# Splitting the 512-column matmuls of one stage into two of 256 columns, in a kernel of Fourier transforms and a feed-forward block

## The chip, the core and the metric

One core of one Trainium2 chip runs the kernel. The metric is the device time of one execution in microseconds (us); the kernel before took 2559.97 us in the median of three runs (2555.99 to 2562.64).

## What is computed

The reference takes x of 8 batches by 3008 places by 256 channels. Along the 3008 places it makes a real Fourier transform, multiplies each frequency by one complex 256 x 256 matrix, adds a bias, pulls real and imaginary parts towards zero by 0.01 and transforms back. A feed-forward block follows on all 24064 rows.

```
X = rfft(x, axis=1)
Yr = Xr @ w_r - Xi @ w_i + b_r
Yi = Xr @ w_i + Xi @ w_r + b_i
Y  = sign(Y) * max(|Y| - 0.01, 0)        (for Yr and Yi)
y  = irfft(Yr + 1j * Yi, n=3008, axis=1)
h  = y @ w_in                            (256 -> 2048)
out = (h * clip(h + 3, 0, 6) / 6) @ w_out  (2048 -> 256)
```

## The kernel before

3008 is 64 times 47, so each transform is made of a 47-point and a 64-point one, and each of these is a matmul with a table of sines and cosines. The work of a batch goes through these steps:

- `stage1`: the forward 47-point transform, 7 loads of x, to a scratch tensor in DRAM (`scr1`).
- `middle`, in 12 groups `g`: `s2` is the forward 64-point transform, `s3` the product with the 256 x 256 weights, the bias and the shrinking, `s4` the split of its result into a high and a low part, and `s5` the inverse 64-point transform, whose result `pt` goes to a second scratch tensor (`scr2`).
- `segment`: the inverse 47-point transform, 7 segments, from `scr2` through the tile `qt` into `raw`.
- The feed-forward block, in 47 chunks of 512 columns, of 8 units each. Its first layer (`phase_a` to `phase_d`, tiles `pb`, `pc`, `pd`) takes seven products of 256 columns in place of eight; its second (`down`, tile `po`) gives each weight to two matmuls of 256 columns.

Most products are made of values split in two (`split`, L133 to L137): a high part of a shorter type and the rest. `product` (L147) then issues three matmuls for each pair of operands: rest times high, high times rest, high times high, all into the same place of PSUM.

The step of the change is `s5` (L494). Batch 0 takes another form. For batches 1 to 7 it issues through `product` three matmuls, each 128 x 128 weights by 512 columns, into one bank of PSUM (`ps_a`, 128 x 512, two buffers): first with the weights `g_lo`, then twice with `g_hi`; the moving operand is the two halves of `z`. That is 84 groups and 252 matmuls. Each matmul has one load of its weights. The flag `whole` hands the three to `together` (L139), which lets no other matmul of TensorE come between them. ScalarE then copies the bank to `pt` (L500), and SyncE's queue stores it (L501).

The order within each engine is not that of the code: a scheduler plans it when the kernel is built, with a model of how long each instruction takes, and writes one list for each engine. The code sets priorities, and the places at which steps of `stage1`, `middle` and `segment` may enter between those of the feed-forward block (`lay`, `fill`). So an instruction whose modelled length changes can change the order of all that comes after it.

Of the kernel before, what the change touches and what calls it, by code (L numbers as in the profile page):

```python
# [101 lines left out]
def spectral_ffn(ctx: ExitStack, tc: tile.TileContext, x, w_r, w_i, bias, w_in, w_out, f47, f64, g64, sgn, out):  # L102
# [12 lines left out]
    def space(shape, dt, name, tag=None):  # L115
        tag = tag or name
        return sb.tile(shape, dt, name=name, tag=tag, bufs=depth.get(tag, 1))
# [6 lines left out]
    def room(wide=False):  # L124
        if wide:
            return ps_b.tile([P, 512], F32, name="pb")
        return ps_a.tile([P, 512], F32, name="ps_a")
# [11 lines left out]
    def together(matmuls):  # L139

        first, *rest = [functools.partial(nc.tensor.matmul, **m) for m in matmuls]
        first = first()  # L142
        with tc.high_priority(), tc.issue_after(first.ins):
            for m in rest:
                m()  # L145

    def product(ps, terms, start=True, stop=True, more=False, whole=False):  # L147

        todo = [p for (ah, al), (bh, bl) in terms for p in ((al, bh), (ah, bl), (ah, bh))]
        matmuls = [  # L150
            dict(
                out=ps,
                lhsT=a,
                rhs=b,
                start=start and n == 0,
                stop=stop and n == len(todo) - 1,
                skip_group_check=more,
            )
            for n, (a, b) in enumerate(todo)
        ]  # L160
        if whole:
            together(matmuls)
        else:
            for m in matmuls:
                last = nc.tensor.matmul(**m)  # L165
            return last
# [133 lines left out]
    def stage1(b):  # L300
# [17 lines left out]
        for i, (n1, n) in enumerate(sets):  # L318
# [8 lines left out]
            for c, src in enumerate((e, plus)):  # L327
                q = 2 * i + c
                if whole:
                    ps = idle(q) if b else room(c == 1)  # L330
                    turns = f47_s[2][:rows, c * R47 : c * R47 + rows]
                    nc.tensor.matmul(out=ps[:rows, :w], lhsT=turns, rhs=src, start=True, stop=True)
                else:
                    xs = [t[:rows, :w] for t in twin([P, 2 * D], F32R, "xs")]
                    split(*xs, src, nc.gpsimd)
                    yield
                    ps = room()
                    product(ps[:rows, :w], [([t[:rows, c * R47 : c * R47 + rows] for t in f47_s[:2]], xs)], whole=True)
                home = ("a", "h", "z", "h", "xs", "h", "X")[q % 7] if b == 0 else "yb" if whole else "a"
                a = space([P, 2 * D], F32, "a", home)[:rows, :w]  # L340
                if home == "X":
                    space([P, 48], F32, "gap")
                nc.scalar.copy(out=a, in_=ps[:rows, :w])
                dst = scr1[b][c, n1 : n1 + n].rearrange("(g j) k d -> (j k) g d", g=w // D)
                stores.append(nc.sync.dma_start(out=dst, in_=a.rearrange("p (g d) -> p g d", d=D)))
                if c and i + 1 < len(sets) and i + 1 >= len(shapes) and not whole:
                    shapes.append(load(i + 1))
                yield
# [40 lines left out]
    g64_s = g64_t[:2]  # L389
# [6 lines left out]
    def middle(b):  # L396
# [5 lines left out]
        bt, xs, zs = {}, {}, {}  # L402

        def tag(g, *tags):

            return tags[0 if b else g % 3]
# [34 lines left out]
        def mixed(ps, x, *terms):  # L441
            product(
                ps,
                [
                    (tuple(t[:, dh, which] for t in x), part(w_s[w], slice(dh * D, (dh + 1) * D)))
                    for which, w in terms
                    for dh in range(2)
                ],
            )
# [42 lines left out]
        def s5(g):  # L492
            ps = room(b == 0)
            flat = lambda t: t.rearrange("p k d -> p (k d)")  # L494
            if b:
                product(ps, [(g64_s, [flat(t) for t in zs.pop(g)])], whole=True)
            else:
                nc.tensor.matmul(out=ps, lhsT=g64_t[2], rhs=flat(zs.pop(g)), start=True, stop=True)
            pt = space([P, 2, D], F32, "pt", tag(g, "pt", "ot", "ot"))
            nc.scalar.copy(out=pt, in_=ps.rearrange("p (k d) -> p k d", d=D))  # L500
            nc.sync.dma_start(out=dst[:, 2 * g : 2 * g + 2, :], in_=pt)  # L501
# [3 lines left out]
        for g in range(NG + LAG[2]):  # L505
            if g >= LAG[2]:
                s5(g - LAG[2])
                yield
            if b and 0 <= g - LAG[1] < NG:
                s4(g - LAG[1])  # L510
            if 0 <= g - LAG[0] < NG:
                s3(g - LAG[0])
            if 0 <= g - LAG[0] < NG + 1:
                yield
            if g < NG:
                s2(g)
                yield
# [73 lines left out]
    def prepare(c):  # L591
        y = raw.pop(c)
        b11, b12, b21, b22 = y[:, 0, :H], y[:, 0, H:], y[:, 1, :H], y[:, 1, H:]
        s = space([P, 4, H], F32, "T")
        for to, p, q in ((0, b12, b11), (1, b22, s[:, 0]), (2, b22, b12), (3, b21, s[:, 1])):
            (nc.gpsimd if c else nc.vector).tensor_tensor(out=s[:, to], in0=p, in1=q, op=ALU.subtract)
        yield
        for n, src in ((2, b21), (1, b11), (6, s[:, 1]), (7, s[:, 2]), (5, s[:, 0]), (4, s[:, 3]), (3, b22)):
            t = space([P, 2, H], F32R, "yb")
            with behind(("h", c * nf - 1 if n == 3 else -1)):  # L600
                split(t[:, 0], t[:, 1], src, nc.gpsimd if c else nc.vector)
            yb[c, n] = (t[:, 0], t[:, 1])
            yield
# [184 lines left out]
    for c in range(1, NC):  # L788
        g = prepare(c)
# [111 lines left out]
```

## Time and profile before

| | before |
|---|---|
| median of three runs | 2559.97 us |
| the profiled execution | 2560.95 us |
| its span, first to last instruction | 2559.2 us |
| TensorE matmuls: busy, number | 2502.8 us (98%), 20910 |
| TensorE weight loads: busy | 2447.6 us (96%) |
| VectorE, ScalarE, GpSimd: busy | 77%, 71%, 30% |
| mean granted TensorE clock | 0.988 |

The profile of one execution lists every instruction with its start and its length. TensorE (PE) has two lists there, matmuls and weight loads (PEld); both are pipelined, so one instruction's length is longer than the distance to the next one's start, and it is the distance that sets the time. "ps_a<-z,g_hi" is a matmul that writes tile `ps_a` from the moving or stationary operands `z` and `g_hi`. L142 and L145 are the two lines of `together`, L165 is `product`, L711 is `down`.

### The profile page before, as it was taken

To read this page: it belongs to the slowest core of one execution; us is meant where nothing else is said; L and a number is where in the kernel's file an instruction comes from. 1 tells how busy PE (TensorE), PEld (TensorE's weight loads), DVE (VectorE), ACT (ScalarE), POOL (GpSimd) and SP (SyncE) were. 2 spreads that over 40 slices of the span, in tenths; PEclk is the share of its full clock that TensorE was granted. 3 is DMA by queue.
4 is the path that set the end of the run, shared out by engine and by line. 5 is a ranking of instruction groups with operands and counts; after the bars stand their busy time and mean duration, and the time that the engine had idled before them with its cause. 6 is when DMAs were issued, how large, how long until landed. Compare 5 with 4: busy or idle time off the path is not lost.

```text
span 2559.2 us, 53456 instructions
## 1 busy us (share of the span) xinstructions
PE 2502.8 (98%) x20910; PEld 2447.6 (96%) x20910; DVE 1965.0 (77%) x3191; ACT 1825.9 (71%) x3587; POOL 756.2 (30%) x738
## 2 busy tenths in 40 slices
PE   6789999999999999999999999999999999999999
PEld 4579999999999999999999999999999999999999
DVE  7778878877787777777787777777777778677766
ACT  5467777777777777777777777777777777777776
POOL 3253342333223332323323333223321221121310
PEclk8889999999999999999999999999999999999999
DMA  7733432332222222333222222222222121110000
GB/s 244 224 88 103 126 103 83 91 91 68 60 84 78 86 72 67 85 86 89 60 75 84 72 79 84 71 78 80 74 78 59 53 66 51 37 41 17 12 18 17
DMA packets 150259, 200.54 MB, mean 78 GB/s; under 512 B 16863, under 2 KB 104215, under 8 KB 150007
## 3 DMA queue, kind: packets, MB, share of 16 engines
q1 hardware_dynamic: 150007, 197.13, 26.7%
q8 instruction: 164, 2.69, 0.5%
q14 instruction: 88, 0.72, 0.1%
HBM read 97.45 MB, written 74.97 MB: 67 GB/s over the span
## 4 chain that ended last, share of the span: by engine, by line
PE 90%; DMA 3%; DVE 3%; ACT 1%; POOL 1%; issue 1%; SPq 1%; ACTq 0%; POOLq 0%; DVEq 0%
PE po L711 38%; PE pb L165 19%; PE pc L165 10%; PE ps_a L145 7%; PE ps_a L165 7%; PE pd L165 5%; PE ps_a L142 3%; DMA xin<-in_x 1%; DMA zt<-tc 1%; DMA qt<-scr 0%; DMA x_lo<-in_x 0%; DVE r L682 0%; ACT r L680 0%; POOL e L325 0%; ACT gs L136 0%
## 5 line engine op out<-in xcount | busy, mean ns | idle before, releaser
L711 PE MATMUL po<-gs,w_out_hi 128*128 128x256 f32 x5984 | 1025.6, 277 | 0.0
L711 PEld LDWEIGHTS po<-gs,w_out_hi 128*128 128x128 f32 x5984 | 839.2, 188 | 1.6
L682 DVE SCALAR_TENSOR_TENSOR r<-r,h 128x1024 f32<-128x1024 f32 x375 | 476.4, 1270 | 269.4 <-ACT r L680 267.4
L711 PE MATMUL po<-gs,w_out_lo 128*128 128x256 f32 x2992 | 594.8, 278 | 0.9 <-ACT gs L136 0.5
L680 ACT ACTIVATE r<-h,three 128x1024 f32<-128x1024 f32 x375 | 433.0, 1155 | 191.5 <-DVE h L621 189.4
L165 PE MATMUL pb<-yb,w_in_hi 128*128 128x256 f32 x3008 | 568.2, 278 | 0.0
L137 DVE TENSOR_TENSOR gs<-r,gs 128x1024 fp32r<-128x1024 f32 x375 | 483.5, 1289 | 90.9 <-ACT gs L136 87.1
L136 ACT CAST gs<-r 128x1024 fp32r<-128x1024 f32 x375 | 394.3, 1051 | 109.3 <-DVE r L682 106.6
L165 PEld LDWEIGHTS pb<-yb,w_in_hi 128*128 128x128 f32 x3008 | 458.1, 189 | 3.1
L711 PEld LDWEIGHTS po<-gs,w_out_lo 128*128 128x128 f32 x2992 | 456.0, 188 | 3.8 <-ACT gs L136 2.2
L165 PE MATMUL pb<-yb,w_in_lo 128*128 128x256 f32 x1504 | 426.3, 286 | 2.0 <-ACT u L616 1.3
L137 POOL TENSOR_TENSOR yb<-T,yb 128x256 fp32r<-128x256 f32 x184 | 168.3, 917 | 841.9 <-ACT yb L136 828.2
L621 DVE TENSOR_TENSOR h<-pc,u 128x256 f32<-128x256 f32 x752 | 314.2, 418 | 113.1 <-PE pc L165 106.8
L616 ACT COPY u<-pb 128x256 f32<-128x256 f32 x752 | 279.5, 373 | 94.4 <-PE pb L165 80.5
L165 PE MATMUL pc<-yb,w_in_hi 128*128 128x256 f32 x1504 | 295.7, 278 | 0.0
L165 PEld LDWEIGHTS pb<-yb,w_in_lo 128*128 128x128 f32 x1504 | 283.5, 189 | 8.7 <-ACT u L616 2.8
L165 PEld LDWEIGHTS pc<-yb,w_in_hi 128*128 128x128 f32 x1504 | 228.9, 189 | 0.7
L165 PE MATMUL pc<-yb,w_in_lo 128*128 128x256 f32 x752 | 214.6, 285 | 4.7 <-DVE h L621 4.6
L616 ACT COPY p<-pb 128x256 f32<-128x256 f32 x376 | 140.1, 373 | 77.0 <-PE pb L165 75.1
L654 ACT COPY h<-pb 128x256 f32<-128x256 f32 x376 | 141.3, 376 | 49.4 <-PE pb L165 47.6
L621 DVE TENSOR_TENSOR h<-pd,p 128x256 f32<-128x256 f32 x376 | 156.6, 417 | 13.9 <-ACT p L616 11.8
L165 PEld LDWEIGHTS pc<-yb,w_in_lo 128*128 128x128 f32 x752 | 141.9, 189 | 9.4 <-DVE h L621 8.1
(165 smaller groups left out, 3939.4 us busy)
## 6 DMA issues: line engine op xcount, KB each, us to landing
bt<-scr SPq DMA_DIRECT2D x96, 256.0 KB, 3.0
scr<-pt SPq DMA_DIRECT2D x96, 256.0 KB, 2.4
zt<-tc SPq DMA_DIRECT2D x376, 64.0 KB, 2.0
out<-ot SPq DMA_DIRECT2D x93, 256.0 KB, 2.3
scr<-a SPq DMA_DIRECT2D x96, 240.0 KB, 2.7
qt<-scr SPq DMA_DIRECT2D x96, 240.0 KB, 3.5
xin<-in_x SPq DMA_DIRECT2D x42, 480.0 KB, 4.4
f<-in_f SPq DMA_DIRECT2D x96, 128.0 KB, 2.8
```

Source lines behind the costliest of these rows:

```text
L136: nc.scalar.copy(out=hi, in_=src)
L137: (on or nc.vector).tensor_tensor(out=lo, in0=src, in1=hi.bitcast(F32), op=ALU.subtract)
L142: first = first()
L145: m()
L165: last = nc.tensor.matmul(**m)
L616: nc.scalar.copy(out=t, in_=ps)
L621: nc.vector.tensor_tensor(out=to, in0=ps, in1=keep.pop((i, n)), op=ALU.add)
L654: marks["h", i] = nc.scalar.copy(out=hs[i][:, 1, :H], in_=pb)
L680: nc.scalar.activation(out=r, in_=h, func=AF.Relu, bias=three, scale=1.0)
L682: nc.vector.scalar_tensor_tensor(out=r, in0=r, scalar=6.0, in1=h, op0=ALU.min, op1=ALU.mult)
L711: last = nc.tensor.matmul(out=pos[dh][half], lhsT=w[:, ft * D + dh * P : ft * D + (dh + 1) * P], rhs=g[:, low, u, cols], start=opens and n ...
```

## The change

`product` gets a flag `paired`, and `s5` sets it for batches 1 to 7. Each 512-column matmul of the group becomes two, for columns 0 to 255 and 256 to 511, which follow each other with the same weights; each of the two has its own weight load. Only the first matmul of the six opens the bank (`start`).

```
-    def product(ps, terms, start=True, stop=True, more=False, whole=False):
+    def product(ps, terms, start=True, stop=True, more=False, whole=False, paired=False):
...
+        if paired:
+            matmuls = [
+                dict(
+                    m,
+                    out=m["out"][:, cols],
+                    rhs=m["rhs"][:, cols],
+                    start=m["start"] and cols.start == 0,
+                    skip_group_check=True,
+                )
+                for m in matmuls
+                for cols in (slice(0, 256), slice(256, 512))
+            ]
         if whole:
             together(matmuls)
...
-                product(ps, [(g64_s, [flat(t) for t in zs.pop(g)])], whole=True)
+                product(ps, [(g64_s, [flat(t) for t in zs.pop(g)])], whole=True, paired=True)
```

The change adds 12 lines above all but the first of the lines that are named here, so that L165 reads L177 in the lists of the changed kernel, L501 L513, L711 L723, and so on.

**TensorE at the first group of batch 1.** The list before, with the semaphores that a matmul waits for in brackets:

```order
L165 MATMUL pb<-yb,w_in_lo 128x256 [waits Activation_49]
L165 MATMUL pb<-yb,w_in_hi 128x256 x2
L142 MATMUL ps_a<-z,g_lo 128x512 [waits Activation_49]
L145 MATMUL ps_a<-z,g_hi 128x512 x2
L165 MATMUL pc<-yb,w_in_lo 128x256 [waits DVE_49]
L165 MATMUL pc<-yb,w_in_hi 128x256 x2
L711 MATMUL po_2205<-gs,w_out_lo 128x256 [waits Activation_49]
```

And of the changed kernel:

```order
L177 MATMUL pb<-yb,w_in_lo 128x256 [waits Activation_49]
L177 MATMUL pb<-yb,w_in_hi 128x256 x2
L142 MATMUL ps_a<-z,g_lo 128x256 [waits Activation_49]
L145 MATMUL ps_a<-z,g_lo 128x256
L145 MATMUL ps_a<-z,g_hi 128x256 x4
L177 MATMUL pc<-yb,w_in_lo 128x256 [waits DVE_49]
L177 MATMUL pc<-yb,w_in_hi 128x256 x2
L723 MATMUL po_2205<-gs,w_out_lo 128x256 [waits Activation_49]
```

Three rows became six at the same place, with the same wait at the first; nothing else moved here, and nothing ahead of this group.

**TensorE at the second group.** Before:

```order
L142 MATMUL ps_a<-z,g_lo 128x512 [waits DVE_49,PE_49]
L145 MATMUL ps_a<-z,g_hi 128x512 x2
L711 MATMUL po_2205<-gs,w_out_hi 128x256 x2
L711 MATMUL po_2210<-gs,w_out_hi 128x256 x2
L165 MATMUL pc<-yb,w_in_lo 128x256 [waits DVE_49]
L165 MATMUL pc<-yb,w_in_hi 128x256 x2
L165 MATMUL pd<-yb,w_in_lo 128x256
L165 MATMUL pd<-yb,w_in_hi 128x256 x2
L165 MATMUL ps_a<-w_r_hi,X 128x256 [waits DVE_49]
```

And now:

```order
L142 MATMUL ps_a<-z,g_lo 128x256 [waits DVE_49,PE_49]
L145 MATMUL ps_a<-z,g_lo 128x256
L145 MATMUL ps_a<-z,g_hi 128x256 x4
L723 MATMUL po_2205<-gs,w_out_hi 128x256
L177 MATMUL pc<-yb,w_in_lo 128x256 [waits DVE_49]
L177 MATMUL pc<-yb,w_in_hi 128x256 x2
L723 MATMUL po_2205<-gs,w_out_hi 128x256
L723 MATMUL po_2210<-gs,w_out_hi 128x256 x2
L177 MATMUL ps_a<-w_r_hi,X 128x256 [waits DVE_49]
```

The product into `pc`, which waits for VectorE, moved ahead of three matmuls of the second layer, and the product into `pd` behind the start of `s3`. Such small moves go on to the end of the list.

**SyncE's queue at the first segment of batch 3.** The names carry buffer numbers; the tensor `scr2_8836` (`scr2_8908` after) holds that batch, and `qt_13189` (`qt_13297`) takes its first two parts. Before:

```order
L501 DMA scr2_8836<-pt_12868 128x512
L732 DMA out_0<-ot_12803 128x512
L531 DMA qt_13189<-scr2_8836 120x2x256
L732 DMA out_0<-ot_12808 128x512
L410 DMA bt_13150<-scr1_9247 128x512
L411 DMA f64_13151<-in_f64 128x256
L531 DMA qt_13189<-scr2_8836 120x2x256
```

And now:

```order
L513 DMA scr2_8908<-pt_12976 128x512
L543 DMA qt_13297<-scr2_8908 120x2x256 x2
L744 DMA out_0<-ot_12913 128x512
L744 DMA out_0<-ot_12908 128x512
L422 DMA bt_13258<-scr1_9319 128x512
L423 DMA f64_13259<-in_f64 128x256
```

Both loads of `qt` now stand ahead of the two stores of the output. Of the 1063 transfers of this queue 91 stand at another place than before, by at most 6 places; on ScalarE it is 1451 of 3589 instructions, by at most 11, on VectorE 1036 of 3193, by at most 9, on GpSimd 32 of 743.

## Rows read from the trace of the kernel before

**Rows 1.** The page, part 1: busy time of each engine.

```profile
PE 2502.8 (98%) x20910; PEld 2447.6 (96%) x20910; DVE 1965.0 (77%) x3191; ACT 1825.9 (71%) x3587; POOL 756.2 (30%) x738
```

**Rows 2.** Busy time by stretch (from:to us), with the granted TensorE clock (PEclk).

```profile
200.00:2205.00 2005.00, 2000.62 (x17055) 1975.17 (x17055) 1568.44 (x2567) 1461.17 (x2898) 609.36 (x585) 1.00 0.27 78
2205.00:2555.00 350.00, 349.30 (x2984) 347.08 (x2982) 243.80 (x371) 244.63 (x453) 67.30 (x74) 1.00 0.07 23
```

**Rows 3.** Waits of TensorE's matmuls from 200 to 2205 us: total, times, longest.

```profile
PE ps_a L145 <- DMA qt<-scr: 1.1, 1, 1.1
PE ps_a L142 <- DVE raw L574: 1.1, 1, 1.1
...
PE ps_a L142 <- DVE r L682: 0.5, 2, 0.3
```

**Rows 4.** Instructions that touch z: count, min/median/max ns; then who waited for them (us, times).

```profile
L145 PEld LDWEIGHTS ps_a<-z,g_hi x168: 187/188/192, 226.1 to 2204.3; 128*128 128x128 f32 x168
L145 PE MATMUL ps_a<-z,g_hi x168: 387/393/403, 226.4 to 2204.6; 128*128 128x512 f32 x168
...
L142 PE MATMUL ps_a<-z,g_lo x84: 388/390/502, 226.1 to 2204.1; 128*128 128x512 f32 x84
...
  ACT pt L500: 11.0, 20
```

**Rows 5.** Timeline of matmuls around one group: start us, us, what.

```profile
503.87 0.39 PE L711 MATMUL po<-gs,w_out_hi 128*128 128x256 f32 x2
504.10 0.28 PE L165 MATMUL pc<-yb,w_in_lo 128*128 128x256 f32 x1
...
504.89 0.39 PE L142 MATMUL ps_a<-z,g_lo 128*128 128x512 f32 x1
505.12 0.62 PE L145 MATMUL ps_a<-z,g_hi 128*128 128x512 f32 x2
505.58 0.28 PE L165 MATMUL pb<-yb,w_in_lo 128*128 128x256 f32 x1
505.70 0.40 PE L165 MATMUL pb<-yb,w_in_hi 128*128 128x256 f32 x2
505.93 0.28 PE L165 MATMUL pb<-yb,w_in_lo 128*128 128x256 f32 x1
506.06 0.39 PE L165 MATMUL pb<-yb,w_in_hi 128*128 128x256 f32 x2
```

**Rows 6.** Timeline of weight loads just ahead of the same group.

```profile
504.33 0.53 PEld L711 LDWEIGHTS po<-gs,w_out_hi 128*128 128x128 f32 x4
504.78 0.19 PEld L142 LDWEIGHTS ps_a<-z,g_lo 128*128 128x128 f32 x1
```

**Rows 7.** Chain of waits in three stretches: start us, us, what.

```profile
505.74 0.71 PE pb L165 x6
...
2176.57 1.02 PE ps_a L165 x9
2177.59 0.68 PE pb L165 x6
...
2274.51 1.81 PE po L711 x16
...
2449.36 1.88 PE po L711 x16
```

**Rows 8.** Groups of matmuls by form: 2262 to 2282, 2482 to 2540, 200 to 2205, 2205 to 2560 us.

```profile
L711 PE MATMUL po<-gs,w_out_hi 128*128 128x256 f32 x66 | 11.5, 276 | 0.0
...
L711 PE MATMUL po<-gs,w_out_hi 128*128 128x256 f32 x162 | 29.3, 281 | 0.0
...
L711 PE MATMUL po<-gs,w_out_hi 128*128 128x256 f32 x4874 | 835.2, 277 | 0.0
...
L711 PE MATMUL po<-gs,w_out_hi 128*128 128x256 f32 x1008 | 172.7, 279 | 0.0
```

**Rows 9.** Waits of SyncE's queue from 200 to 2560 us.

```profile
SPq L531 <- PE pb L165: 232.7, 26, 25.4
...
SPq L732 <- ACT ot L729: 138.2, 24, 42.0
```

## The prediction

> **What bounds the kernel now.** I began with the busy times of the engines [rows 1]: TensorE's matmuls fill 98% of the span, its weight loads 96%, VectorE 77%. A share alone doesn't say that TensorE is the limit, so the stretches come next [rows 2]. From 200 to 2205 us, which holds every group that changes (the first matmul of them starts at 226.1, the last at 2204.6 [rows 4]), matmuls are under way for 2000.62 of 2005 us. What is left, 4.4 us, is made of single waits of about a microsecond [rows 3]. After 2205 it is 349.30 of 350. The granted clock is 1.00 in both, the 2.4 GHz level, so there is no clock to win or lose while TensorE stays as busy as that. The reader should see that nothing else matters here: time changes only if the distance between starts of TensorE's matmuls changes, or if TensorE waits more or less.
>
> So the number to read is that distance, not the length in the tables. A 256-column matmul is 276 ns long [rows 8], but sixteen of them take 1.81 us in the chain [rows 7]: 0.113 us each. In the timeline, seven of 256 columns lie between 504.10 and 504.89, again 0.113 each; the three of 512 columns take from 504.89 to 505.58, 0.69 us or 0.230 each [rows 5]. A 512-column matmul therefore takes twice a 256-column one and a little more: both go by columns.
>
> There is a second pace: elsewhere sixteen of the same matmuls take 1.88 us, 0.118 each [rows 7]. The mean length tells which pace a stretch had: 276 ns at 0.113, 281 at 0.118 [rows 8]. From 200 to 2205 it is 277, mostly the short pace; after 2205 it is 279, so over half at the long one.
>
> **The change, part by part.**
>
> *The 252 matmuls become 504.* A group takes 0.69 us now; six at 0.113 take 0.68. That is 0.01 less for each of 84 groups: **-0.9 us**.
>
> *The matmuls behind a group.* After the three of 512 columns, the next four of 256 take from 505.58 to 506.06, 0.48 us where four at 0.113 take 0.45 [rows 5]; in the chain the six behind a group take 0.71 where six take 0.68 elsewhere [rows 7]. So each group leaves some 0.03 us behind it. A group of 256-column matmuls does not: behind the nine of `s3` the six into `pb` take 0.68 [rows 7]. If the new groups behave like those, 84 x 0.03 = **-2.5 us**. The other bound is 0, should the trail come from the bank or from `z` and not from the width. I take -2.5, as the nine of `s3` write the same tile and differ in the width.
>
> *The 252 added weight loads.* One is 188 ns long [rows 4]. If none were hidden they would cost 252 x 0.188 = 47 us; if all are, 0. Four loads in a row take 0.53 us in all [rows 6], 0.188 and three times 0.113, so a load overlaps the one before it and keeps pace with 256-column matmuls. More than 17,000 pairs run that way [rows 2], and I take **0**. The cover is thin: weight loads are under way for 1975 of 2005 us [rows 2].
>
> *The long pace.* I can't see what ends it; it may be an interruption of the even stream, such as a 512-column matmul. A mean of 277 between 276 and 281 puts up to a fifth of 2005 us at the long pace, which costs 0.2 x 2005 x (1 - 0.113/0.118) = 17 us; the trails are 2.5 of that. Groups of 512 columns also stand in `stage1`, and the short ones of `s2` and `segment` interrupt as well, so the group of `s5` is one of four kinds. Were the long stretches a third longer, it would cost +4 to +5; the lower bound is 0. I take **+1**, near the lower end, since those of the trails cannot grow.
>
> *The order.* The planner's lists differ from the second group on, by a few places on each engine. ScalarE's copy to `pt` waited for the group 20 times, 11.0 us in all [rows 4], and stands right behind it as before. Of SyncE's queue, a load of `qt` that stands behind a store waits for the store's own wait first (24 waits of stores for ScalarE, 138.2 us in all, as against 232.7 for `qt` on TensorE [rows 9]). At the first segment of batch 3 both loads now precede the stores, which can only bring `qt` earlier, and the stores wait for nothing later on. But TensorE waited for `qt` once in 2005 us, 1.1 us [rows 3], so little can be won. Elsewhere such a wait can appear. I take **0**, with -5 (all idle time gone) to +5 (as much again) as bounds.
>
> The sum is -0.9 - 2.5 + 0 + 1 + 0 = -2.4 us. The profiled execution took 2560.95 us, so 2558.5; the median of the three runs is 1.0 below that execution, and by it the sum is 2557.6. I forecast **2558 us**.
>
> *A rule that speaks against the change.* The row gives 0.113 against 0.230 us, so two halves cost no more than the whole. The Trainium skill, page "TensorE: Matmul & The Clock Gate", section "Back-to-back issue gap", gives a warm matmul its columns at 2.4 GHz and 2.5 ns on top, so every split pays 2.5 ns again; by that page's figures my estimate is that the 252 splits cost +0.6 us in place of -0.9, and the sum would be 1.5 us higher. The trace disagrees with its figures (0.113 where it has 0.109, 0.230 where it has 0.216), and I go by the trace.
>
> **The rivals.**
>
> 1. *The long pace holds on (slower).* If the 512-column groups are what returns TensorE to the short pace, then without 84 of them it stays long after each disturbance. For it: after 2205 us, where none of these groups stand, over half of the time is at the long pace [rows 8]. Against: that stretch also lacks `s2`, `s3` and `stage1`. If half of 2005 us ran at it, 0.5 x 85 = 42 us would be lost, 2600 us in all. It decides from 8 us on, which is a further tenth of the 2005 us at the long pace; I would then expect about 2570.
>
> 2. *The new order is luckier (faster).* The long stretches after 2205 us cost 0.6 x 350 x 0.042 = 9 us, and the idle time in the two stretches is 5 us. An order that by chance enters the long pace less often at the end and drops the waits gives up to -14 beside the -3.4 above: 2544; half of it, 2550. For it: the order there does change. Against: it may as well go the other way, and is not aimed at.
>
> 3. *The loads are not hidden (slower).* Each second half waits for its own load. The price is up to 47 us, 2606; at half of that 2582. Against it stand the four loads in 0.53 us [rows 6]. The skill's page, in the same section, also has a sustained figure for streams of load and matmul, 131 ns at 512 columns against 81 at 128; an estimate from that page, read linearly, is 98 at 256, so that a split costs 64 ns, 16 us for 252, or 2577. The 0.230 us for 512 columns [rows 5] contradicts it.
>
> 4. *Nothing happens.* If the trail stays, or the repeated load of the same weights behaves as the single one did, the time is 2559 to 2561, no change. For it: by columns the work is the same.
>
> **How the numbers follow.** About 0.3%, 7.7 us, is what a measurement of this kernel can tell from no change; the three runs lie within 6.7 us of each other. My forecast has 0.63, and nothing happening 0.22, both within that bound. Rival 1 has 0.06 and rival 3 has 0.02, both slower by more. Rival 2 has 0.07; the larger part of it, or the whole with the gain above, is faster by more. That gives faster 0.07, same 0.85, slower 0.08. The range runs from 2551, where rival 2 begins to be large, to 2566, which takes in the order's +5 and some of the long pace's +4.
>
> **What would show it.** In the profile after, the six matmuls of a group should take 0.68 us, and the next six 0.68 where it was 0.71; the count of matmuls and loads should be 21162 each, and the loads 188 ns long. The mean length from 200 to 2205 us should stay at 276 to 277 ns: if it rises to 278 or more, rival 1 is right, and the chain will show 1.88 us for sixteen in the middle of the run. If TensorE's idle time there is over 10 us, the order is to blame. A group of over 0.8 us would mean rival 3.

## The result, and the profile after

The changed kernel takes 2571.17 us in the median of five runs (2569.45 to 2574.7), the kernel before 2557.7 us in five runs beside them (2555.99 to 2562.64): a ratio of 1.0054, 95% interval 1.0042 to 1.0065. The change makes the kernel slower by some 13.5 us, which lies outside the range that was forecast. The profiled executions lie closer together, 2570.76 against 2560.95 us, since that of before was one of its longer ones.

Page, part 1, and busy time by stretch of the changed kernel (columns as in [rows 2]):

```profile
PE 2505.9 (98%) x21162; PEld 2463.4 (96%) x21162; DVE 1969.1 (77%) x3191; ACT 1827.1 (71%) x3587; POOL 764.2 (30%) x738
```

```profile
200.00:2205.00 2005.00, 1999.74 (x17185) 1985.99 (x17185) 1565.03 (x2547) 1452.98 (x2876) 606.49 (x577) 1.00 0.27 78
2205.00:2565.00 360.00, 358.12 (x3091) 354.74 (x3089) 251.45 (x388) 253.27 (x474) 78.32 (x81) 1.00 0.07 22
```

The 252 added matmuls and loads are there. TensorE is as busy as before [rows 2] and its clock is at the same level, 1.00. It should have done more in 2005 us if nothing had got slower: 84 groups bring 252 more instructions, but only 130 more lie in that stretch than before. Idle time is 5.3 us where it was 4.4. So the loss is in the distance between matmuls while TensorE counts as busy.

Timeline of matmuls around one group, answering to [rows 5]:

```profile
506.33 0.62 PE L723 MATMUL po<-gs,w_out_hi 128*128 128x256 f32 x4
506.78 0.28 PE L142 MATMUL ps_a<-z,g_lo 128*128 128x256 f32 x1
506.89 0.28 PE L145 MATMUL ps_a<-z,g_lo 128*128 128x256 f32 x1
507.01 0.62 PE L145 MATMUL ps_a<-z,g_hi 128*128 128x256 f32 x4
507.46 0.28 PE L177 MATMUL pb<-yb,w_in_lo 128*128 128x256 f32 x1
507.58 0.40 PE L177 MATMUL pb<-yb,w_in_hi 128*128 128x256 f32 x2
507.82 0.28 PE L177 MATMUL pb<-yb,w_in_lo 128*128 128x256 f32 x1
507.93 0.40 PE L177 MATMUL pb<-yb,w_in_hi 128*128 128x256 f32 x2
508.17 0.28 PE L177 MATMUL pd<-yb,w_in_lo 128*128 128x256 f32 x1
```

The six matmuls of the group take from 506.78 to 507.46, 0.68 us: 0.113 each, as forecast. The six behind it take from 507.46 to 508.17, 0.71: 0.118 each. So far this is the trail of before. But it doesn't end. The chain of waits in the same place, and later in the run:

```profile
507.62 0.71 PE pb L177 x6
508.33 0.35 PE pd L177 x3
508.69 0.71 PE ps_a L177 x6
509.39 0.35 PE pc L177 x3
509.75 1.53 PE po L723 x13
...
1948.14 1.89 PE po L723 x16
```

Nine matmuls into `ps_a` and `pc` behind it take 1.06 us and thirteen into `po` 1.53, all at 0.118; around 1948 us sixteen take 1.89, where [rows 7] have 1.81 and 1.88 for the two paces. The groups of matmuls by form say the same of whole stretches, 200 to 2205 us and then 2205 us to the end (answering to the last two lines of [rows 8]):

```profile
L723 PE MATMUL po<-gs,w_out_hi 128*128 128x256 f32 x4835 | 834.0, 278 | 0.0
...
L723 PE MATMUL po<-gs,w_out_hi 128*128 128x256 f32 x1045 | 177.3, 277 | 0.0
```

The mean rose from 277 to 278 in the first and fell from 279 to 277 in the second. A mean of whole nanoseconds is too coarse for a price, so I counted the distances between the starts in the timeline, for 256-column matmuls. I call 116 to 130 ns the long pace, take its cost as what is over 113.3 ns, and count all above 130 ns as waits:

| | long pace, 190 to 2205 us | its cost | long pace, 2205 to 2555 us | its cost | waits, cost in both |
|---|---|---|---|---|---|
| before | 1435 of 15323 | 6.9 us | 1669 of 2877 | 7.5 us | 30.4 us |
| after | 4758 of 15715 | 21.8 us | 659 of 2909 | 3.0 us | 32.9 us |

The long pace costs 14.9 us more where the groups are and 4.5 less behind them, and waits 2.5 more; the three are 12.9 us. What lies outside the table (matmuls of other widths, the start and the end of the run) gives some 3 us back. The difference of the two profiled executions is 9.8.

Where the long pace begins and ends can be counted by groups. I take the groups behind which at least 14 matmuls of the feed-forward block follow before a group of another stage. Such a group leaves the long pace behind if most of the seventh to fourteenth distances there are long, and it found the long pace if most of the six distances of the feed-forward block ahead of it were long. From 190 to 2205 us, 1 of 50 groups of `s5` left the long pace behind before, and 39 of 53 do after. It ends at two other stages: of the groups that found it in the changed kernel, all 12 of `stage1` and all 12 of `segment` left the short pace behind, but only 1 of 26 of `s3`.

### The profile page after: what moved, and what is told of

Read it like the earlier page. It is cut to its first block, busy times and chain, and to the rows that moved or that the text cites. A ratio compares the mean times of both kernels' runs of the same rounds, so it can differ in the third digit from the quotient of the medians.

```text
span 2569.0 us, 53979 instructions
## 1 busy us (share of the span) xinstructions
PE 2505.9 (98%) x21162; PEld 2463.4 (96%) x21162; DVE 1969.1 (77%) x3191; ACT 1827.1 (71%) x3587; POOL 764.2 (30%) x738
## 4 chain that ended last, share of the span: by engine, by line
PE 91%; DMA 3%; DVE 2%; ACT 2%; POOL 1%; issue 1%; SPq 0%; ACTq 0%; DVEq 0%
PE po L723 39%; PE pb L177 19%; PE pc L177 10%; PE ps_a L145 8%; PE ps_a L177 7%; PE pd L177 5%; PE ps_a L142 3%; DMA zt<-tc 1%; DMA x_lo<-in_x 0%; DVE r L694 0%; DMA xin<-in_x 0%; ACT r L692 0%; DMA st<-in_w_out 0%; DVE w_in_lo L137 0%; POOL m L242 0%
## 5 line engine op out<-in xcount | busy, mean ns | idle before, releaser
L723 PE MATMUL po<-gs,w_out_hi 128*128 128x256 f32 x5984 | 1029.3, 277 | 0.0
L723 PEld LDWEIGHTS po<-gs,w_out_hi 128*128 128x128 f32 x5984 | 841.2, 188 | 0.7
L694 DVE SCALAR_TENSOR_TENSOR r<-r,h 128x1024 f32<-128x1024 f32 x375 | 482.7, 1287 | 253.1 <-ACT r L692 251.5
L723 PE MATMUL po<-gs,w_out_lo 128*128 128x256 f32 x2992 | 597.0, 278 | 1.5 <-ACT gs L136 1.1
L177 PE MATMUL pb<-yb,w_in_hi 128*128 128x256 f32 x3008 | 571.9, 278 | 0.0
L177 PEld LDWEIGHTS pb<-yb,w_in_hi 128*128 128x128 f32 x3008 | 459.1, 189 | 1.6
L723 PEld LDWEIGHTS po<-gs,w_out_lo 128*128 128x128 f32 x2992 | 456.4, 188 | 4.2 <-ACT gs L136 3.2
L177 PE MATMUL pb<-yb,w_in_lo 128*128 128x256 f32 x1504 | 427.1, 286 | 3.5 <-ACT u L628 2.3
L177 PE MATMUL pc<-yb,w_in_hi 128*128 128x256 f32 x1504 | 296.5, 278 | 0.0
L177 PEld LDWEIGHTS pb<-yb,w_in_lo 128*128 128x128 f32 x1504 | 283.6, 189 | 8.5 <-ACT u L628 4.2
L177 PEld LDWEIGHTS pc<-yb,w_in_hi 128*128 128x128 f32 x1504 | 229.3, 189 | 0.6
L177 PE MATMUL pc<-yb,w_in_lo 128*128 128x256 f32 x752 | 214.6, 285 | 8.0 <-DVE h L633 7.9
L137 POOL TENSOR_TENSOR xs<-xin,xs 120x512 fp32r<-120x512 f32 (+1 forms) x45 | 60.4, 1341 | 328.2 <-ACT xs L136 320.8
```

Source lines behind the costliest of these rows:

```text
L137: (on or nc.vector).tensor_tensor(out=lo, in0=src, in1=hi.bitcast(F32), op=ALU.subtract)
L694: nc.vector.scalar_tensor_tensor(out=r, in0=r, scalar=6.0, in1=h, op0=ALU.min, op1=ALU.mult)
L723: last = nc.tensor.matmul(out=pos[dh][half], lhsT=w[:, ft * D + dh * P : ft * D + (dh + 1) * P], rhs=g[:, low, u, cols], start=opens and n ...
```

## The experiments

Three theories stood at the start. A: something in or behind a split group leaves TensorE at the long pace. B: another property of the group does (its operands, its length). C: the planner's new order causes it through waits. Each expectation says anew what A, B and C stand for in its run. The runs of the kernel before beside the experiments had medians of 2558.16, 2556.78 and 2557.12 us in the three sets.

### First set: order, width and stage

**The halves in turn.** All three products for columns 0 to 255, then all for 256 to 511:

```
-                for m in matmuls
                 for cols in (slice(0, 256), slice(256, 512))
+                for m in matmuls
```

> The six matmuls of a group in another order: columns 0 to 255 with g_lo, g_hi, g_hi, then columns 256 to 511 with g_lo, g_hi, g_hi, so that no weights are loaded four times in a row and the halves of the bank don't alternate. Theory A (a group of 256-column matmuls with these operands leaves TensorE at the 0.118 us pace, whatever their order): about 2571 us, and the matmuls behind a group stay at 0.118. Theory B (the pace is set off by the alternating halves or the repeated weights): about 2557 us, and the matmuls behind a group run at 0.113. Theory C (the planner's new order costs the 13 us through waits, the pace is a by-thing): 2566 to 2574, as the order is nearly that of the change, with waits of TensorE 3 us or more above the kernel before.

2569.26 us, ratio 1.0047 (1.0032 to 1.0063). Neither the alternating halves nor the weights repeated four times matter; the theories A and C are left, as both expected this time.

**The last matmul left whole.**

```
-                for m in matmuls
+                for m in matmuls[:-1]
                 for cols in (slice(0, 256), slice(256, 512))
-            ]
+            ] + [dict(matmuls[-1], skip_group_check=True)]
```

> Only the first two matmuls of a group are split; the third stays at 512 columns. Theory A (a 512-column matmul at the end of a group lets TensorE return to 0.113 after some five matmuls, a 256-column one doesn't): 2555 to 2560 us, and a trail of about five slower matmuls as in the kernel before. Theory B (any split of the group sets off the long pace and nothing at its end helps): about 2571. Theory C (the planner's order): 2565 to 2573.

2574.78 us, ratio 1.0066 (1.0051 to 1.0081), the opposite of what theory A expected. Chain of waits around one group, five matmuls of which the last has 512 columns:

```profile
608.92 0.11 PE ps_a L142
609.03 0.57 PE ps_a L145 x4
609.60 0.35 PE po L723 x3
...
610.07 0.35 PE pc L177 x3
610.42 0.59 PE pb L177 x5
611.01 0.59 PE po L723 x5
```

Sixteen matmuls later TensorE is still at 0.118. A 512-column matmul does not bring the short pace back by its width. That part of rival 1's explanation does not hold for this group.

**Both stages split**, the groups of `stage1` as well, so that no 512-column matmul is left in batches 1 to 7:

```
-                    product(ps[:rows, :w], [...], whole=True)
+                    product(ps[:rows, :w], [...], whole=True, paired=w == 512)
```

> The change, and also the 512-column matmuls of stage1 in batches 1 to 7 (26 groups of three in two thirds of the batches, 78 groups in all) are split in the same way. Theory A (512-column groups are what ends the long pace in the middle of the run): the long pace lasts longer, 2580 to 2595 us, mean matmul length from 200 to 2205 us at 279 or more. Theory B (each split group changes the pace from one to the other, also back): more changes but about as much time at either, 2568 to 2580. Theory C (order alone): within 5 us of the change, 2566 to 2576.

2579.01 us, ratio 1.008 (1.0064 to 1.0097): at the upper end of B's range and 1 us short of A's, whose sign, a mean of 279, doesn't come (it is 278). 6265 of 16080 distances up to 2205 us are at the long pace. The split groups of `stage1` end it less often: 10 of the 14 that found it, where it was 12 of 12.

**Only `stage1` split**, the groups of the inverse transform as before.

> The kernel before with the 512-column matmuls of stage1 split in place of those of the inverse 64-point transform. Theory A (a split group of any stage leaves TensorE at 0.118): slower than before, 2565 to 2572 us, and the matmuls behind a stage1 group run at 0.118. Theory B (the operands of the inverse transform, g and z, set it off, not the width): 2555 to 2560 us, and 0.113 behind a stage1 group, without the trail. Theory C (order alone): 2553 to 2570, either way.

2557.1 us, ratio 1.0003 (0.9993 to 1.0012). Splitting 512 columns costs no time that the interval shows in the other stage: six matmuls into `ps_a` with `xs` leave a trail of three or four and no more. The chain around one such group:

```profile
499.05 0.12 PE ps_a L142
499.17 0.59 PE ps_a L145 x5
499.76 0.58 PE pb L177 x5
500.34 0.45 PE po L723 x4
500.79 0.11 PE pb L177
500.90 1.70 PE po L723 x15
```

The fifteen at the end are at 0.113. So it is not width alone but something about the group of `s5`.

### Second set: places in SBUF

What differs are the operands, and they differ in one thing that no row shows: where they stand. As the tiles are laid out, the weights of the feed-forward layers and, in batches 1 to 7, `X`, the stationary operand of `s3`, start at 160 modulo 256 bytes, and their moving operands (`yb`, `gs`, the 256 x 256 weights) at 96. In the group of the change it is the other way round: `g_hi` and `g_lo` at 96, `z` at 160. Two pads in the code can be moved to change that without touching any instruction. The pad behind `g64` goes ahead of it, and the order in which batch 0 first asks for three tiles decides on which side of the other pad `z` stands:

```
+        const.tile([P, 16], F32, name="last")
         g64_t = loaded(g64, P, P, "g64")
         nc.sync.dma_start(out=sgn_s, in_=sgn)
-        const.tile([P, 16], F32, name="last")
...
-                home = ("a", "h", "z", "h", "xs", "h", "X")[q % 7] if b == 0 else ...
+                home = ("a", "h", "X", "h", "z", "h", "xs")[q % 7] if b == 0 else ...
```

The operations of TensorE, ScalarE and SyncE are then, row for row, those of the kernel from which it is made, so the planner's order is held fixed. The first hunk alone is the first run of this set, the second alone the fourth, both together the second and, on the kernel before, the third.

> The change with one thing moved in SBUF: the tables g_hi, g_lo stand 64 bytes later, at 160 modulo 256 bytes, where the weights of the feed-forward layers and of s3 stand too; z stays at 160. The order on every engine is that of the change, row for row. Theory A (where stationary and moving operand stand in SBUF sets the pace: elsewhere weights are at 160 and the moving operand at 96, in this group it is the other way round, and each such turn switches between 0.113 and 0.118): something changes behind the groups; if the two together count, the group is now half turned and the time lies anywhere from 2553 to 2571; if the weights alone count, 2553 to 2560. Theory B (the operands g and z in themselves, or the length of the group): 2567 to 2573. Theory C (the planner's order): 2567 to 2573, as the order is the same.

> The change with z (and xs) at 96 modulo 256 bytes, g_hi and g_lo left at 96; the order on every engine is that of the change. Theory A: if the two together count, half turned, 2553 to 2571; if the moving operand alone counts, 2552 to 2560 and the first of these runs stays at 2571; if the weights alone count, 2567 to 2573. Theory B and theory C: 2567 to 2573.

> The change with g_hi, g_lo at 160 modulo 256 bytes and z at 96, as weights and moving operands stand in the other groups; xs moves to 96 too, other tiles but X keep their places, and the order on every engine is that of the change. Theory A (places in SBUF): no change of pace behind a group, 2552 to 2559 us, mean matmul length from 200 to 2205 us back at 276 to 277. Theory B (the operands or the length of the group): 2567 to 2573. Theory C (the planner's order): 2567 to 2573.

> The kernel before, 512 columns in a group, with the same places as the last: g_hi, g_lo at 160, z and xs at 96 modulo 256 bytes; its order on every engine is its own. Theory A (places): the trail of some five slower matmuls behind a group goes as well, 84 times some 0.02 to 0.03 us, 2553 to 2558 us. Theory B (the trail comes from 512 columns): trail and time as before, 2556 to 2561. Theory C says nothing of it but no change.

| columns in a group | g at, z at (modulo 256) | median us | ratio to before, interval | long pace, 190 to 2205 us |
|---|---|---|---|---|
| 256 (the change) | 96, 160 | 2571.17 | 1.0054, 1.0042 to 1.0065 | 4758 of 15715 |
| 256 | 160, 160 | 2561.39 | 1.0014, 1.0004 to 1.0024 | 2166 of 15806 |
| 256 | 160, 96 | 2557.76 | 0.9999, 0.9988 to 1.001 | 1932 of 15797 |
| 256 | 96, 96 | 2575.08 | 1.0072, 1.0055 to 1.0089 | 5847 of 15665 |
| 512 (before) | 96, 160 | 2556.78 | 1 | 1435 of 15323 |
| 512 | 160, 96 | 2573.6 | 1.0064, 1.0048 to 1.008 | 4904 of 15184 |

The chain of waits behind a group with both moved, 256 columns:

```profile
525.47 0.11 PE ps_a L142
525.58 0.57 PE ps_a L145 x5
526.15 0.68 PE pb L177 x6
526.83 0.34 PE pd L177 x3
527.17 0.34 PE pc L177 x3
527.51 2.38 PE po L723 x21
```

Everything behind it here runs at 0.113: no trail, and no long pace. With the same matmuls in the same order as the change, 64 bytes in the places of the operands take the 13.5 us away. That settles it against theory C. The same places under the kernel before do the opposite; the chain behind a group of three 512-column matmuls:

```profile
527.55 0.23 PE ps_a L142
527.77 0.47 PE ps_a L145 x2
528.24 0.71 PE pb L165 x6
528.95 0.35 PE pd L165 x3
529.30 0.35 PE pc L165 x3
529.65 1.41 PE po L711 x12
```

Now the unsplit group stays at 0.118. I had expected its trail to go, and it became endless: a miss, and the most telling run. At these places the split is worth 2573.6 - 2557.8 = 16 us; at the places of before it costs 13.5. The value of the change has no sign of its own.

The rows of the table with 256 columns tell more than their times. Here are the group and a piece behind it with `g` alone moved, and then with `z` (and `xs`) alone moved:

```profile
527.36 0.59 PE ps_a L145 x5
...
529.33 1.25 PE po L723 x11
```

```profile
531.11 0.60 PE ps_a L145 x5
...
533.12 0.94 PE po L723 x8
```

In both the group itself is slow, 0.118 or more per matmul; in the median it takes 0.707 and 0.717 us, where it takes 0.682 with the operands at 96 and 160 and 0.680 at 160 and 96. So in the two rows where both stand at the same place, the group has the long pace; most of its own matmuls are then among the long ones of the table. But what it leaves behind differs: 0.114 with `g` alone moved, 0.118 with `z` alone moved. Counted as above, 2 of 53 groups leave the long pace with `g` alone moved and 3 of 53 with both moved, but 40 of 53 with `z` alone moved and 39 of 53 with neither. At the places tried, what a split group leaves behind goes by `g` and not by `z`. Of the unsplit groups 1 of 50 leave it at 96 and 160, and 36 of 50 at 160 and 96; which of the two operands counts there was not run.

### Third set: is there a rule, and a faster kernel?

**`z` moved, `xs` not**: the order of first use is ("a", "h", "xs", "h", "X", "h", "z"), with the weights' pad moved.

> As the run with both moved (g_hi, g_lo at 160 modulo 256 bytes, z at 96), but xs, the moving operand of stage1, stays at 160 as in the kernel before; the order is that of the change. Theory A (places): no change of pace behind a group of the inverse transform; behind a stage1 group the trail of the kernel before (about 120, 118, 119, 116 ns); 2553 to 2560 us. If xs at 96 had been what brought the time down, it would be 2567 to 2573.

2557.13 us, ratio 0.9996 (0.9986 to 1.0006). So it was `g` and `z`, not `xs`; 1 of 54 groups leaves the long pace behind. Long pace up to 2205 us: 1379 of 15835, as few as before; behind the groups no trail is left. The 2.5 us that the trail should be worth don't show: waits cost 35.5 us here against 30.4.

**The tables of `stage1` moved too**, to 32 modulo 128 bytes, with all behind them 128 bytes later:

```
+    sgn_s = const.tile([P, NK], F32, name="sgn")
+    f47_s = []
+    for t, dt in (("hi", F32R), ("lo", F32R), ("all", F32)):
+        f47_s.append(const.tile([R47, 2 * R47], dt, name="f47_" + t))
+        if t == "hi":
+            const.tile([P, 16], F32, name="pad_hi")
...
     bias_s = const.tile([P, 2 * D], F32, name="bias")
-    sgn_s = const.tile([P, NK], F32, name="sgn")
+    const.tile([P, 16], F32, name="pad_bias")
```

> As the run with both moved, and the tables of the forward 47-point transform (f_hi, f_lo) at 32 modulo 128 bytes, where the other weights stand; all tiles behind them 128 bytes later, so that what is the same modulo 128 stays so; the order is that of the change. Theory A with a period of 128 bytes: the feed-forward layers keep 0.113, the stage1 groups, still 512 columns, either return to it as now or, as the 512-column group of the inverse transform did at these places, don't: 2553 to 2558 in the first case, 2565 to 2575 in the second. If the period is 256 bytes or more, w_in and yb are now out of step and most of the run goes at 0.118: over 2600 us.

2564.41 us, ratio 1.0026 (1.0017 to 1.0035): in neither range, nearest to the second. The long pace now begins elsewhere: 43 of 60 groups of `segment` and 40 of 54 of `s2` leave it behind, where with both operands moved it was 1 of 60 and 3 of 53. The table `f_all`, the moving operand of `segment`, is one of those moved, so this run changed that stage too.

**And `bt`, the stationary operand of `s2`, moved by 64 bytes**:

```
+            if b == 0 and g == 0:
+                space([P, 16], F32, "gap_bt")
+            data = space([P, 2, D], F32, "bt")
+            if b == 0 and g == 0:
+                space([P, 16], F32, "gap_f64")
-            bt[g] = space([P, 2, D], F32, "bt"), space([P, 2, P], F32, "f64")
+            bt[g] = data, space([P, 2, P], F32, "f64")
...
-                    space([P, 48], F32, "gap")
+                    space([P, 16], F32, "gap")
```

> As the last run, and bt, the stationary operand of the forward 64-point transform, at 32 modulo 128 bytes in place of 96, with its moving operand at 96 as before; the order is that of the change. Theory A: fewer entries into the 0.118 pace behind those groups, 0 to 3 us below the last run. If these places don't matter for 128-column matmuls: the same as the last run within 2 us.

2612.05 us, ratio 1.0211 (1.0197 to 1.0224), far from what any theory expected. From 200 to 2205 us:

```profile
L733 PE MATMUL po<-gs,w_out_hi 128*128 128x256 f32 x4749 | 830.3, 280 | 0.0
```

A mean of 280, close to the 281 of the long pace alone; 11665 of 15429 distances are long. The last hunk shortens a pad, by which `yb`, `z` and the other tiles between the pads go back to their old places modulo 256 while `w_out`, `gs` and `X` stay 128 bytes on. So this run moved more than one relation at once, and can't say which of them costs the 48 us.

**All split, all moved**, the run with the `stage1` tables moved and `stage1` split as well.

> As the run with the stage1 tables moved, and the 512-column matmuls of stage1 split too, so that no 512-column matmul is left in batches 1 to 7; the order is that of the run with both stages split, which took 2579 us. Theory A (256-column groups with weights at 32 and moving operands at 96 modulo 128 bytes don't change the pace): 2550 to 2556 us, no trail behind either kind of group, the long pace only behind waits. Theory B (a 512-column group is needed to end the long pace): 2570 to 2580 as before the move. Theory C (the planner's order): about 2579.

2568.64 us, ratio 1.0044 (1.0031 to 1.0056): 10 us less than with both stages split at the old places and the same order, but slower than before. My rule "weights at 32, moving operands at 96 modulo 128 bytes, 256 columns" holds for the group of the change, of which 5 of 52 leave the long pace behind, and not for the kernel: 26 of 55 split groups of `stage1` do, and 49 of 61 of `segment`.

## Why the prediction was wrong

- **What bounds the kernel** was right: TensorE's distances decide, not its waits. The two paces were seen and priced in [rows 7, 8].
- **The 252 matmuls**, -0.9 us: right in sign, and rounded up. A group takes 0.682 us in the median where it took 0.688, and all 84 together 58.7 us where they took 59.1: -0.4 us.
- **The matmuls behind a group**, -2.5 us: this step failed. I argued that the nine of `s3` leave no trail, that they write the same tile and differ only in the width. They also differ in where their operands stand, which the rows don't name. The trail became longer instead of going: 39 of 53 groups leave the long pace behind, and with `g` moved by 64 bytes 2 of 53. My other bound was 0, "should the trail come from the bank or from `z`"; nothing above 0 was allowed for.
- **The 252 weight loads**, 0: right. Loads have their 0.188 us and a group keeps 0.113 per matmul.
- **The long pace**, +1 us: mis-sized. It is +14.9 us up to 2205 us and -4.5 behind it, the trails included. I took it that the trails can't grow.
- **The order**, 0: right within its bounds. Waits cost 2.5 us more, and the run with both operands moved has that order and the time of before.
- **Rival 1** had the place, the sign and the size, 2570 us, and a chance of only 0.06. Its cause was wrong: it is not that 84 groups are missing that would end the long pace, but that the split groups begin it. The groups of `s5` had nothing to end in the kernel before, as none of the 32 whose approach can be counted found the long pace; what ends it are groups of `stage1`, most of them of 512 columns, and of `segment`, of 120 columns or fewer. One 512-column matmul at the end of a group changed nothing (2574.78 us), three of them leave the long pace behind at other places (2573.6), and 256-column groups leave the short pace alone at those (2557.76). The sign that I gave for it, a mean of 278 from 200 to 2205 us, came out, but it can't tell the two causes apart.
- **Rivals 2 to 4**: of rival 2 a part came, as the long pace costs 4.5 us less behind 2205 us; why is not shown. Rival 3 is out, as a group takes 0.68 us, far below 0.8, and so is rival 4, by the time. Idle time is 5.3 us, below the 10 that would have blamed the order.

What makes TensorE keep one of two paces, and which relation between the places counts over all stages, stays open. The runs show only that 64 bytes decide it for `g` and `z`, for the split group in the place of `g` alone, and that the answer turns round between 256 and 512 columns.

## What to carry to other kernels

Where TensorE is the bound, read the distance between the starts of its matmuls, stretch by stretch, before the shares of busy time: a slower pace hides in a share that doesn't change. A term won from "these other matmuls don't do it" holds only if they are alike in width, in operands and in where these stand; give it a bound on the other side of zero. And before a split or a merge of matmuls is judged, run it with its operands moved by 64 bytes: here the same split was worth -16 us or +13.5.

## What the runs showed of the hardware

- A stream of 256-column matmuls of these split values has two paces, 0.113 and 0.118 us, at a granted clock of 1.00. In the changed kernel it keeps the short one for up to 216 of them and the long one for up to 396, counted up to 2205 us with waits and other widths left out. Groups of some stages switch the pace (39 of 53 split groups of `s5` leave the long one, all 12 of `stage1` that found it the short one), others keep it (25 of 26 of `s3`).
- The places of the two operands in SBUF decide whether a group switches the pace: 64 bytes for `g` and `z` moved the kernel between 2557.8 and 2575.1 us with the same order on the engines, and other pads took it to 2612.05 us.
- With those pads 11665 of 15429 distances up to 2205 us were long. No version beat the kernel before by more than the intervals hold, the best being 0.9996 (0.9986 to 1.0006).
